# Mixed-head attention with a rational feed-forward layer: the order of the score products spread anew

## The chip, the cores and the metric

The kernel runs on one core of a Trainium2 chip. The metric is the device time in microseconds of one execution. In this document PE is TensorE's matmul stream and PEld its weight loads, DVE is VectorE, ACT is ScalarE, POOL is GpSimd, and SP is SyncE, whose queue issues most DMAs.

## The reference, cut to what matters

```python
# q, k, v: (4, 12, 448, 64); w_pre, w_post: (12, 12)
scores = scale * np.matmul(q, k.transpose(0, 1, 3, 2))
scores = np.einsum('bhij,hg->bgij', scores, w_pre)       # first mix over heads
scores = scores - np.max(scores, axis=-1, keepdims=True)
attn = np.exp(scores)
attn = attn / (np.sum(attn, axis=-1, keepdims=True) + 1e-09)
attn = np.einsum('bhij,hg->bgij', attn, w_post)          # second mix over heads
attn = np.matmul(attn, v)
# x = attn as (1792, 768); w_in: (768, 2048); w_out: (2048, 768)
h = x @ w_in
g = (a0 + a1*h + a2*h**2 + a3*h**3) / (1 + abs(b0)*abs(h) + abs(b1)*h**2 + 1e-6)
out = g @ w_out
```

All of it is in float32.

## The kernel before

**Attention.** The 448 query rows of each of the 4 batches are cut into four tiles, three of 120 rows and one of 88 (the first of batch 0, the last of the other batches), 16 tiles in all. A tile's scores are made two heads at a time: `put_qk` (line 498, weight loads and matmuls on 64x64 quarters of the array) writes a pair of heads into the two PSUM banks `ps_s`, ACT or DVE copies each head to a staging buffer `st` (helper lines 236 and 238), and a DMA from SP's queue (line 520) scatters it into `d`, where heads and ten query rows lie side by side on the partitions. There are two buffers `d`, one for even and one for odd tiles, two banks `ps_s` (one pair of heads at a time) and six staging buffers (three pairs). So a tile's six pairs are made while the tile before is worked on, and the scatter into a `d` waits until the last first mix of two tiles before has read it.

A tile is worked on in groups of two blocks of ten rows: six groups for 120 rows, five for 88. For each group g:

- `put_pre` ("pre", line 599, quarters): the first mix from `d` into a PSUM pair, `ps_t` or `ps_u`; then DVE takes the negated maximum (line 605), ACT two exps with their sums (line 614), POOL and DVE the reciprocals, and POOL scales the weights of the second mix (line 634).
- `put_post` ("post", line 674, 64x32 eighths), two groups later (`LAG = 2`): the second mix into the two banks `ps_a`, which DVE transposes into `aa` (line 690).
- `put_av` (line 739, quarters): the products of a tile with V, in three parts at groups 2, 3 and 4 of the next tile, summed in the one of `ps_t`, `ps_u` that the first mix leaves free meanwhile. For these groups, and the one behind them, the first mix has one PSUM pair only and so waits for the exps of the group before it. After the third part ACT and DVE take the sums to `xs`.

**The order.** A planner (`Plan`) takes every operation with an estimated duration and a due time (`at`), and writes out each engine's instructions in the order in which its list scheduling starts them. On TensorE it isn't free in the attention part: each call of `pe` is tied behind the one before, so the order is that of the calls. The loop over g at the end sets it: pre(g), then the score pairs in `early[g]`, then post(g-2), then AV, then the pairs in `late[g]`. `PLACES` says for a tile of five or six groups where the next tile's six pairs go: a place i is group i // 2, counted from that tile's first group, early where i is even, late where it is odd. Copies of scores go to ACT or DVE, whichever the planner finds free first.

**Feed-forward.** 64 units follow: 18 matmuls (line 918) into `ps_s`, the rational function on ACT and DVE, 18 matmuls (line 1008) into `ps_t`, `ps_u` and `ps_a`. The feed-forward weights are converted from 8-byte numbers during both parts (lines 406 to 450).

Of the kernel before, what the change touches and what calls it, by code (L numbers as in the profile page):

```python
# [54 lines left out]
class Plan:  # L55
# [11 lines left out]
    def add(self, eng, dur, fn, deps=(), at=0.0, extra=0.0, since=0.0, after=(), mode=None, late=0.0):  # L67
        op = Op(eng, dur, fn, [d for d in deps if d is not None], at, extra, since, mode, late)
        op.behind = list(after)
        self.ops.append(op)  # L70
        return op
# [124 lines left out]
def dve(n, fast=False):  # L196
    return 0.16 + 0.53e-3 * n if fast else 0.14 + 1.06e-3 * n
# [6 lines left out]
def copies(n, sb=True, on=("act", "dve")):  # L204
    return {e: act(n, sb) if e == "act" else dve(n, sb) for e in on}
# [23 lines left out]
def place(i, h):  # L229

    return STRIDE * i + EDGE + h


def move(nc, eng, o, i):
    if eng is nc.scalar:
        eng.copy(o, i)  # L236
    else:
        eng.tensor_copy(o, i)  # L238
# [3 lines left out]
def mixed_attention_then_rational_ffn(ctx: ExitStack, tc, q, k, v, w, wmix, mask, a, b2, out):  # L242
# [59 lines left out]
    tau = [T0]  # L302
# [3 lines left out]
    first = {}  # L306
# [177 lines left out]
    def put_qk(T, pr, at, ps_="s"):  # L484

        n, b = rows[T], T // 4
        box = {}

        def mm():
            if ps_ in "sa":  # L490
                box["s"] = [bank(ps_), bank(ps_)]
            else:
                pair = both(ps_)
                box["s"] = [pair[:, 0], pair[:, 1]]
            for i0, i1 in ((0, 64), (64, TQ)):
                for hh in range(2):
                    d = slice(64 * hh, 64 * hh + 64)
                    nc.tensor.matmul(  # L498
                        box["s"][hh][i0:i1, 0:S], lhsT=Q[T][d, pr, i0:i1], rhs=K[b][d, pr, :], start=True, stop=True)

        def copy(hh):
            def fn(eng):
                if T in STAGE:
                    if T not in staged:
                        t = sb[STAGE[T]].tile([128, 12 * S], F32, tag=STAGE[T], name="st0")
                        staged[T] = t.rearrange("p (h s) -> p h s", h=12)
                    box[hh] = staged[T][0:TI, 2 * pr + hh, :]
                else:
                    box[hh] = sb["st"].tile([TI, S], F32, tag="st", name="st")
                move(nc, eng, box[hh][0:n], box["s"][hh][0:n, 0:S])  # L510
            return fn

        def other(h):
            return T == 0 and h in (1, 3, 5)

        def shuffle(h):
            def fn():
                Dt[T] = d_sb[T % 2]
                p0 = place(0, h)
                (nc.scalar if other(h) else nc.sync).dma_start(  # L520
                    out=Dt[T][p0:p0 + STRIDE * (G10 - 1) + 1:STRIDE, 0:nblk[T], :], in_=box[h % 2][0:n])
            return fn

        slots = [R["ps_" + ps_].take() for _ in range(2)]
        o = pe(0.82, mm, [q_ld[T], k_ld[b][pr * len(k_ld[b]) // (H // 2)]] + slots, at=at, extra=0.16, mode="quarters")
        qk_op[T, pr] = o
        for hh in range(2):
            h = 2 * pr + hh
            home = R[STAGE.get(T, "st")]
            after = []  # L530
            if T not in STAGE or h == 0:
                free = [home.take()]
            else:
                free, after = [], [first_copy[T]]
            on = ON["s"] if T > 1 else ON["s"] if T else ("act",) if other(h) else ("dve",)
            c = add(copies(S, False, on=on), 0, copy(hh), [o, *free], at=at, after=after)
            if h == 0:
                first_copy[T] = c
            if other(h):
                c.behind.extend(shuf[0][-2:-1] if h > 1 else ())  # L540
            R["ps_" + ps_].uses[slots[hh].k].append(c)
            st_use = home.uses[0 if T in STAGE else -1]
            deps, after = [c], []
            if h == 0:
                deps += [R["d"].take(), clear[T] if T < 2 else None]
            else:
                after.append(shuf[T][0])
            if T == 1:
                after.extend(s for s in shuf[0])
            s_ = add("act" if other(h) else "sp", 0.85, shuffle(h), [x for x in deps if x], at=at - (1.0 if other(h) else 0.0), extra=0.95 * n / TI, after=after)  # L550
            st_use.append(s_)
            shuf.setdefault(T, []).append(s_)
            on_right.append(s_)
        if pr == H // 2 - 1:
            R["q"].uses[T].append(o)
        R["k"].uses[b].append(o)
# [3 lines left out]
    def pe(dur, fn, deps, at, extra, mode=None):  # L560

        op = add("pe", dur, fn, deps, at=at, extra=extra, after=pe_last[-1:], mode=mode)
        pe_last.append(op)
        return op
# [92 lines left out]
    def put_post(g, at):  # L657

        T, kb = groups[g]
        box, o4, e_use, _ = posts[g]
        nt, m = len(box), nblk[T]
        banks = [{}, {}]

        def post():
            for c in range(2):
                banks[c]["p"] = bank("a")
            for r in range(nt):
                for jh in range(2):  # L670
                    for m_ in range(2):
                        for c in range(2):
                            p, q_ = slice(64 * c, 64 * c + 64), BT * (2 * m_ + jh)
                            nc.tensor.matmul(  # L674
                                banks[c]["p"][q_:q_ + BT, JH * r:JH * (r + 1)], lhsT=box[r]["kr"][p, m_, :],
                                rhs=box[r]["e"][p, JH * jh:JH * (jh + 1)], start=True, stop=True)

        def turn(c):
            def fn():
                if kb == 0 and c == 0:  # L680
                    t = sb["a"].tile([128, NB * BT * (TI // G5)], F32, tag="a", name="aa")
                    A[T] = t.rearrange("q (b s p) -> q b s p", b=NB, p=BT)
                src = banks[c]["p"][:, 0:nt * NB * BT]
                if nt == 2:
                    o = A[T][:, :, kb + c:kb + c + m + 1:m, :].rearrange("q b r p -> q r b p")
                    src = src.rearrange("q (r b p) -> q r b p", r=2, b=NB)
                else:
                    o = A[T][:, :, c * m + kb, :]
                    src = src.rearrange("q (b p) -> q b p", b=NB)
                nc.vector.transpose(o, src)  # L690
            return fn

        slots = [R["ps_a"].take() for _ in range(2)]
        o5 = pe(0.77, post, o4 + slots, at, 0.1, "eighths")
        for u in e_use:
            u.append(o5)
        for c in range(2):
            deps, after = [o5], []
            if kb == 0 and c == 0:
                deps.append(R["a"].take())  # L700
            else:
                after.append(evac[T][0])
            o6 = add("dve", dve(nt * NB * BT), turn(c), deps, at=at + 1.0, after=after)
            R["ps_a"].uses[slots[c].k].append(o6)
            evac.setdefault(T, []).append(o6)
# [102 lines left out]
    for pr in range(H // 2):  # L808
        put_qk(1, pr, at=-2.0 + pr, ps_="uastua"[pr])
    early, late = {}, {}  # L810
    PLACES = {5: (-2, -1, 0, 2, 3, 4), 6: (-2, 0, 2, 4, 5, 6)}
    for T in range(2, NT):
        for pr, i in enumerate((-4, -3, -2, 3, 4, 5) if T == 2 else PLACES[first[T] - first[T - 1]]):
            (late if i % 2 else early).setdefault(first[T - 1] + i // 2, []).append((T, pr))
    avs = {}
    for T in range(NT):
# [9 lines left out]
    for g in range(-1, len(groups) + LAG + 4):  # L826
        if 0 <= g < len(groups):
            put_pre(g)
        for T, pr in early.get(g, ()):
            put_qk(T, pr, at=tau[g] + 0.9)  # L830
        if 0 <= g - LAG < len(groups):
            put_post(g - LAG, at=tau[g] + 1.8)
        for T, pr in avs.get(g, ()):
            put_av(T, pr, at=tau[g] + 3.6)
        for T, pr in late.get(g, ()):
            put_qk(T, pr, at=tau[g] + 3.5)
    for i in range(len(VIA) * NCV):
        g = first[1] + 6 + (first[NT - 1] - first[1] - 3) * i // (len(VIA) * NCV)
# [254 lines left out]
    for u in range(len(units)):  # L1093
        i = u + PH * NCV
# [65 lines left out]
```

## Time and profile before

| | |
|---|---|
| median of 3 runs | 833.24 us (831.55 to 838.17) |
| the profiled execution | 822.94 us, span 821.2 us |
| TensorE's granted clock, mean | 0.998 |
| PE, PEld busy | 97%, 73% of the span |
| DVE, ACT, POOL busy | 84%, 61%, 27% |
| stretch of attention | until about 340 us |

The profile is of one execution. Its times are from the start of its span. A row of the order of time merges instructions of one kind that follow each other; its start is that of the first. The place behind a bracket's arrow is what the profile takes for the event that ended the idle time before the first of them; "issue" means that no event is known.

### The profile page before, as it was taken

The numbers are of one execution on the slowest core, as the hardware profiler recorded it, in microseconds if no ns is written. First come the engines' busy times: TensorE is split into PE (matmuls) and PEld (weight loads), VectorE is DVE, ScalarE is ACT, GpSimd is POOL, SyncE is SP. The second block draws the span as 40 slices with busy tenths as digits, with TensorE's granted clock in tenths as the row PEclk, the third lists the DMA queues.
The fourth block names the chain that finished last, engine by engine and source line by source line (L and its number), as shares of the span: only waits on it lengthen the run. The fifth ranks groups of instructions, "written<-read, shape, count | busy, mean of one in ns | idle before, by whom it ended". The sixth has DMA issues, their size and how long they took to land.

```text
span 821.2 us, 23269 instructions
## 1 busy us (share of the span) xinstructions
PE 799.4 (97%) x9368; PEld 598.1 (73%) x9368; DVE 692.3 (84%) x1252; ACT 502.0 (61%) x1099; POOL 223.7 (27%) x394
## 2 busy tenths in 40 slices
PE   7899999999999999999999999999999999999998
PEld 2245555554454454689999999999999999999997
DVE  6777788888887888788999998999989998777775
ACT  2557666656665666666777776677657676545632
POOL 2334444434343445611211212222212222100000
PEclk9999999999999999999999999999999999999999
DMA  6777887668877865974733275656467534466314
GB/s 219 254 215 235 259 280 236 209 199 281 266 212 210 269 192 189 352 243 192 257 126 100 75 255 126 188 124 125 84 215 212 152 81 67 94 221 224 128 52 157
DMA packets 72332, 155.46 MB, mean 189 GB/s; under 512 B 12608, under 2 KB 53152, under 8 KB 71072
## 3 DMA queue, kind: packets, MB, share of 16 engines
q1 hardware_dynamic: 68468, 142.47, 52.6%
q0 software_dynamic: 3456, 11.01, 8.2%
q8 instruction: 74, 1.21, 0.6%
q10 hardware_dynamic: 300, 0.48, 0.2%
q14 instruction: 34, 0.28, 0.1%
HBM read 77.49 MB, written 37.75 MB: 140 GB/s over the span
## 4 chain that ended last, share of the span: by engine, by line
PE 87%; DVE 5%; DMA 3%; ACT 2%; issue 1%; POOL 1%; SPq 0%; ACTq 0%; POOLq 0%; DVEq 0%
PE ps_s L918 29%; PE ps_u L1008 10%; PE ps_t L1008 9%; PE ps_a L1008 9%; PE ps_s L498 8%; PE ps_a L674 8%; PE ps_u L599 4%; PE ps_t L599 4%; PE ps_u L739 3%; PE ps_t L739 2%; ACT e L614 2%; DVE nm L605 2%; DMA d<-st 1%; DVE aa L690 1%; DMA kk<-in_k 1%
## 5 line engine op out<-in xcount | busy, mean ns | idle before, releaser
L690 DVE STREAM_TRANSPOSE aa<-ps_a 128x448 f32<-128x448 f32 (+1 forms) x184 | 107.7, 618 | 11.7 <-PE ps_a L674 11.2
L918 PE MATMUL ps_s<-d,w 128*128 128x448 f32 x504 | 107.3, 366 | 0.0
L918 PE MATMUL ps_s<-xs,w 128*128 128x448 f32 x504 | 107.1, 366 | 0.0
L447 POOL TENSOR_TENSOR w<-cm,w 128x384 fp32r<-128x384 f32 x48 | 56.0, 1167 | 171.9 <-ACT w L236 165.0
L918 PEld LDWEIGHTS ps_s<-d,w 128*128 128x128 f32 x504 | 94.3, 188 | 8.8 <-issue 0.7
L918 PEld LDWEIGHTS ps_s<-xs,w 128*128 128x128 f32 x504 | 94.6, 188 | 7.9
L634 POOL TENSOR_SCALAR krs<-kpost,rr 128x64 f32<-128x64 f32 x180 | 80.8, 462 | 69.2 <-DVE rr L625 48.0
L674 PEld LDWEIGHTS ps_a<-e,krs 64*32 64x32 f32 x2880 | 44.9, 106 | 74.7 <-issue 26.6
L674 PE MATMUL ps_a<-e,krs 64*32 64x224 f32 x2880 | 93.2, 355 | 1.5 <-DVE aa L690 0.8
L236 ACT COPY st<-ps_s 120x448 f32<-120x448 f32 (+1 forms) x115 | 57.6, 533 | 57.8 <-PE ps_s L498 30.5
L931 ACT ACTIVATE m<-ps_s,a_sb 128x448 f32<-128x448 f32 x64 | 46.3, 723 | 76.1 <-PE ps_s L918 72.7
L498 PE MATMUL ps_s<-kk,q 64*64 64x448 f32 x696 | 90.2, 548 | 0.3 <-DVE st L238 0.3
L1008 PE MATMUL ps_u<-g,w 128*128 128x448 f32 x336 | 84.1, 366 | 0.0
L1008 PE MATMUL ps_a<-g,w 128*128 128x448 f32 x336 | 84.1, 366 | 0.0
L1008 PE MATMUL ps_t<-g,w 128*128 128x448 f32 x336 | 83.9, 366 | 0.0
L614 ACT ACTIVATE e<-ps_t,nm 128x448 f32<-128x448 f32 x92 | 57.7, 634 | 31.1 <-DVE nm L605 28.0
L614 ACT ACTIVATE e<-ps_u,nm 128x448 f32<-128x448 f32 x88 | 55.2, 633 | 28.9 <-DVE nm L605 24.6
L1008 PEld LDWEIGHTS ps_t<-g,w 128*128 128x128 f32 x336 | 63.1, 188 | 5.3
L1008 PEld LDWEIGHTS ps_a<-g,w 128*128 128x128 f32 x336 | 63.1, 188 | 5.2
L1008 PEld LDWEIGHTS ps_u<-g,w 128*128 128x128 f32 x336 | 63.1, 188 | 5.2
L961 DVE TENSOR_TENSOR sq<-sq,ua 128x448 f32<-128x448 f32 x64 | 41.4, 648 | 19.4 <-ACT ua L958 19.1
L954 ACT ACTIVATE ua<-sq 128x448 f32<-128x448 f32 x64 | 37.1, 580 | 33.9 <-DVE sq L951 33.6
(94 smaller groups left out, 1445.1 us busy)
## 6 DMA issues: line engine op xcount, KB each, us to landing
d<-st SPq DMA_DIRECT2D x144, 210.0 KB
cr<-in_w SPq DMA_DIRECT2D x64, 384.0 KB
d<-x_scr SPq DMA_DIRECT2D x5, 2688.0 KB
xs<-x_scr SPq DMA_DIRECT2D x4, 2688.0 KB
o_scr<-o POOLq DMA_DIRECT2D x24, 448.0 KB, 5.5
d<-st SPq DMA_DIRECT2D x45, 157.5 KB
x_scr<-xs SPq DMA_DIRECT2D x12, 540.0 KB
q<-in_q SPq DMA_DIRECT2D x16, 384.0 KB
```

The lines of the kernel that those rows point to most:

```text
L236: eng.copy(o, i)
L447: eng.tensor_sub(t[:, 1, :], box["m"].bitcast(F32), t[:, 0, :].bitcast(F32))
L498: nc.tensor.matmul(box["s"][hh][i0:i1, 0:S], lhsT=Q[T][d, pr, i0:i1], rhs=K[b][d, pr, :], start=True, stop=True)
L599: nc.tensor.matmul(box[r if nt == 2 else 0]["t"][64 * c:64 * c + 64, 0:S], lhsT=kpre[p], rhs=Dt[T][p, kb + c if nt == 2 else kb, :], start ...
L614: nc.scalar.activation(e, box[r]["t"][:, 0:S], AF.Exp, bias=box[0]["nm"][:, r:r + 1], accum_out=box[0]["sm"][:, r:r + 1])
L634: eng.tensor_scalar_mul(box[r]["kr"], kpost, rr)
L674: nc.tensor.matmul(banks[c]["p"][q_:q_ + BT, JH * r:JH * (r + 1)], lhsT=box[r]["kr"][p, m_, :], rhs=box[r]["e"][p, JH * jh:JH * (jh + 1)], ...
L690: nc.vector.transpose(o, src)
L918: nc.tensor.matmul(h[:, 0:S], lhsT=W[fi][:, wi, kk * 128:(kk + 1) * 128], rhs=x[:, kk // 3, xj, kk % 3, :], start=(n == 0), stop=(n == 3 * ...
L931: nc.scalar.activation(new("m"), box["h"], AF.Identity, scale=a_sb[:, 3:4], bias=a_sb[:, 2:3])
L961: nc.vector.tensor_mul(box["vv"], box["vv"], box["rc"])
L1008: nc.tensor.matmul(O[key][:, 0:S], lhsT=W[fi][:, wi, DM + m * 128:DM + (m + 1) * 128], rhs=box["g"][:, gi, :], start=(f == 0 and n == 0), ...
```

## The change

The places of the pairs of heads, given as group within the tile that is worked on (a minus counts back from its first group; a tile's pairs begin in the tile before):

| | before | after |
|---|---|---|
| six groups | -1, 0, 1, 2, 2 late, 3 | -2 late, -1, 0, 1, 2, 3 |
| five groups | -1, -1 late, 0, 1, 1 late, 2 | -2 late, -1, 0, 1, 1 late, 2 |
| tile 1 (scores of tile 2) | -2, -2 late, -1, 1 late, 2, 2 late | -2, -2 late, -1, 1, 2, 3 |

In a row of six-group tiles each group then has one pair, the fifth group's behind its AV. And a group whose predecessor has a late pair has its own early pairs behind its post instead of ahead of it, with a due time 0.9 us later.

```diff
-    PLACES = {5: (-2, -1, 0, 2, 3, 4), 6: (-2, 0, 2, 4, 5, 6)}
+    PLACES = {5: (-3, -2, 0, 2, 3, 4), 6: (-3, -2, 0, 2, 4, 6)}
     for T in range(2, NT):
-        for pr, i in enumerate((-4, -3, -2, 3, 4, 5) if T == 2 else PLACES[first[T] - first[T - 1]]):
+        for pr, i in enumerate((-4, -3, -2, 2, 4, 6) if T == 2 else PLACES[first[T] - first[T - 1]]):
             (late if i % 2 else early).setdefault(first[T - 1] + i // 2, []).append((T, pr))
...
     for g in range(-1, len(groups) + LAG + 4):
         if 0 <= g < len(groups):
             put_pre(g)
-        for T, pr in early.get(g, ()):
+        swap = g - 1 in late
+        for T, pr in () if swap else early.get(g, ()):
             put_qk(T, pr, at=tau[g] + 0.9)
         if 0 <= g - LAG < len(groups):
             put_post(g - LAG, at=tau[g] + 1.8)
+        for T, pr in early.get(g, ()) if swap else ():
+            put_qk(T, pr, at=tau[g] + 1.8)
         for T, pr in avs.get(g, ()):
             put_av(T, pr, at=tau[g] + 3.6)
         for T, pr in late.get(g, ()):
```

## Rows read from the trace of the kernel before

**Rows 1.** Stretches: a tile of attention, and 200 us of feed-forward.
```profile
core 0: us, PE busy (x) PEld busy (x) DVE busy (x) ACT busy (x) POOL busy (x), PEclk, DMA share, GB/s
75.60:96.50 20.90, 20.61 (x464) 10.35 (x456) 16.71 (x32) 14.34 (x39) 9.18 (x20) 1.00 0.77 237
...
400.00:600.00 200.00, 200.00 (x986) 184.75 (x985) 189.88 (x343) 137.04 (x260) 44.89 (x41) 1.00 0.49 138
```

**Rows 2.** Order of time, PEld: groups 0 to 5 of tile 5.
```profile
start us, us, engine line op out<-in xcount [idle before <-releaser]
117.27 0.21 PEld L599 LDWEIGHTS ps_t<-d,kpre 64*64 64x64 f32 x8 [0.36 <-PE ps_a L674]
...
122.44 0.21 PEld L599 LDWEIGHTS ps_t<-d,kpre 64*64 64x64 f32 x8 [0.36 <-ACT st L236]
...
124.10 0.56 PEld L674 LDWEIGHTS ps_a<-e,krs 64*32 64x32 f32 x32 [0.70 <-POOL krs L634]
125.02 1.47 PEld L739 LDWEIGHTS ps_u<-aa,vv 64*64 64x64 f32 x56 [0.36 <-ACT st L236]
126.44 0.25 PEld L498 LDWEIGHTS ps_s<-kk,q 64*64 64x64 f32 x8
...
129.15 0.56 PEld L674 LDWEIGHTS ps_a<-e,krs 64*32 64x32 f32 x32 [0.70 <-issue]
...
131.46 0.29 PEld L599 LDWEIGHTS ps_t<-d,kpre 64*64 64x64 f32 x8
132.46 0.14 PEld L674 LDWEIGHTS ps_a<-e,krs 64*32 64x32 f32 x2 [0.70 <-issue]
...
135.36 0.21 PEld L599 LDWEIGHTS ps_t<-d,kpre 64*64 64x64 f32 x8
...
138.26 0.24 PEld L599 LDWEIGHTS ps_u<-d,kpre 64*64 64x64 f32 x8 [0.68 <-PE ps_a L674]
```

**Rows 3.** Order of time, PEld: the same load, of group 5, in tile 10.
```profile
239.88 0.21 PEld L599 LDWEIGHTS ps_t<-d,kpre 64*64 64x64 f32 x8 [0.30 <-ACT e L614]
```

**Rows 4.** Order of time, ACT: the last exp of group 2 in rows 2.
```profile
126.25 0.22 ACT L614 ACTIVATION_READ_ACCUMULATOR e<-ps_t,nm 128x1 f32 x1
```

**Rows 5.** Order of time, PEld: pair, pre, pair at the seam to tile 11.
```profile
242.46 0.47 PEld L498 LDWEIGHTS ps_s<-kk,q 64*64 64x64 f32 x8 [0.36 <-ACT st L236]
...
244.43 0.43 PEld L498 LDWEIGHTS ps_s<-kk,q 64*64 64x64 f32 x8 [0.74 <-DVE st L238]
245.56 0.56 PEld L674 LDWEIGHTS ps_a<-e,krs 64*32 64x32 f32 x32 [0.70 <-issue]
```

**Rows 6.** Order of time, DVE and ACT: the copies at that seam.
```profile
242.64 1.17 DVE L690 STREAM_TRANSPOSE aa<-ps_a 128x448 f32<-128x448 f32 x2
243.75 0.62 DVE L238 COPY st<-ps_s 120x448 f32<-120x448 f32 x1
...
243.46 0.62 ACT L614 ACTIVATE e<-ps_t,nm 128x448 f32<-128x448 f32 x1
...
244.07 0.53 ACT L236 COPY st<-ps_s 120x448 f32<-120x448 f32 x1
```

**Rows 7.** Order of time, PEld: pair, pre, pair in the two five-group tiles.
```profile
165.40 0.44 PEld L498 LDWEIGHTS ps_s<-kk,q 64*64 64x64 f32 x8 [0.36 <-ACT st L236]
...
169.12 0.37 PEld L674 LDWEIGHTS ps_a<-e,krs 64*32 64x32 f32 x24 [0.70 <-issue]
...
249.06 0.47 PEld L498 LDWEIGHTS ps_s<-kk,q 64*64 64x64 f32 x8 [0.36 <-ACT st L236]
...
253.21 0.56 PEld L674 LDWEIGHTS ps_a<-e,krs 64*32 64x32 f32 x32 [0.70 <-POOL krs L634]
```

**Rows 8.** Order of time, PEld: pair, pre, pair in tile 1.
```profile
38.51 0.21 PEld L498 LDWEIGHTS ps_s<-kk,q 64*64 64x64 f32 x8 [0.36 <-ACT e L614]
...
41.66 0.56 PEld L674 LDWEIGHTS ps_a<-e,krs 64*32 64x32 f32 x32 [0.71 <-POOL krs L634]
```

**Rows 9.** Order of time, ACT, and the chain of waits: two waits for scatters.
```profile
251.72 0.53 ACT L236 COPY st<-ps_s 120x448 f32<-120x448 f32 x1 [1.21 <-DMA d<-st]
...
213.28 4.56 DMA d<-st
```

## The prediction

> **What bounds the kernel now.** I read three views in this order: the table of stretches, TensorE's weight loads in order of time, and DVE's and ACT's instructions at the places where those loads wait. In the feed-forward part nothing waits: TensorE is busy 200.00 of 200 us there, and the attention part is busy 20.61 of 20.90 us in a typical tile [rows 1]. So the end follows TensorE's order of work, and what the attention part gains or loses is passed on one to one to the end.
>
> The busy share hides the waits that matter. The weight loads show them, because a load that must wait starts late while earlier matmuls still stream. Attention runs in groups of two block pairs; a full group is a first mix ("pre"), a pair of heads' scores, a second mix ("post"). In the cycle of rows 2, two full groups take 122.44 - 117.27 = 5.17, or 2.58 each. Of that, pre and scores take 124.10 - 122.44 = 1.66 and post 125.02 - 124.10 = 0.92; a value product (AV) takes 126.44 - 125.02 = 1.42; a pre without scores 132.46 - 131.46 = 1.00 [rows 2]. So one pair of heads costs 0.66 us of TensorE's path in a place where nothing waits.
>
> The whole six-group cycle is 138.26 - 117.27 = 20.99. Two places of it hold waits that the change touches. (a) Pair, pre, pair in a row (from the load at 126.44 to the post at 129.15) takes 2.71, against 1.66 + 0.66 = 2.32 without a wait: 0.39 too long. Both score banks are in use, and the second pair needs the two copies of the first. (b) The group with no scores lasts 135.36 - 131.46 = 3.90, while its work is 1.00 + 0.92 + 1.42 = 3.34: 0.56 idle [rows 2]. The pre that follows takes the PSUM pair of the group before and waits for its exps; in another tile the same load shows it by name, with 0.30 us idle and "ACT e" as releaser [rows 3].
>
> By the Trainium skill (Perfetto Trace Analysis, Identifying the Most-Contended Engine) matmul busy time is a poor measure of headroom and weight-load busy time a better one. The trace agrees: the tile of rows 1 leaves 0.3 us by matmul busy time and has 10.35 of 20.90 us of weight loads. By matmul busy time the whole change could win about 4 us over 13 tiles; by the loads' starts several times that.
>
> **The change part by part.** Nothing is added or removed: the same 96 pairs, with the same matmuls, copies and scatter DMAs. In a six-group tile the pairs stood 1, 1, 2, 1, 0, 1 over groups 0 to 5; now each has one, that of group 4 behind its AV, that of group 5 behind its post. The number of changes between the mixes' two array shapes stays at 12 per tile, as each group keeps one post with other work on both sides.
>
> Six-group tiles (11 that hold a full set), each term per tile:
> - Place (a) goes: minus 0.39 [rows 2].
> - Place (b) is filled by the late pair: 3.34 + 0.66 = 4.00 against 3.90 for the same group, so the 0.56 of idle time goes and the pair nearly fits into it. Minus 0.56.
> - Groups 2 and 3 shrink to 1.66 + 0.92 + 1.42 = 4.00. But their exps bound them: the last exp of the group that began at 122.44 ends at 126.25 + 0.22 = 126.47 [rows 4], 4.03 later, and a release must still reach TensorE. I take 0.07 each: plus 0.14. Below it is zero, above it 0.5 each if copies delay the exps further.
> - The pair of group 5, now behind post, stands directly ahead of group 0's pre and pair: a new pair, pre, pair. The row that is nearest is the same place in the tiles ahead of a five-group tile, where a second pair already stood behind post of group 5: from 242.46 to 245.56 is 3.10, against 2.32, so 0.78 [rows 5]. It is long because the first pair's two copies queue behind other work: on DVE the copy at 243.75 follows two transposes (242.64, 1.17), on ACT that at 244.07 follows an exp [rows 6], and the second pair's load starts at 244.43 after 0.74 idle. In the new order these transposes and exps are also due there, so I take this row and not the 2.71 of place (a), whose copies met idle engines. Plus 0.78; bounds 0.39 (a) and 1.83 (the worst row, below).
>
> Sum: -0.39 - 0.56 + 0.14 + 0.78 = -0.03 a tile, nothing over 11 tiles. The end of the cycle stays as busy as it was: it has the late pair's copies in addition to the evacuation of the AV sums, both on ACT and DVE.
>
> Five-group tiles (2 that hold scores). Here pair, pre, pair at groups 1 and 2 is the worst of the trace: 253.21 - 249.06 = 4.15 and 169.12 - 165.40 = 3.72 [rows 7]. With group 2's pair behind post the second pair is a whole post further from the first, which leaves 2.32 for the same pieces: -1.83 and -1.40. The group without scores, which sat idle for exps, gets a pair as in (b), worth about 0.3 [rows 3] in each. Together -3.8.
>
> Tile 1 (scores of tile 2 at groups 1, 2, 3 in place of 1, 2, 2): its pair, pre, pair of 41.66 - 38.51 = 3.15 [rows 8] goes, -0.83. Its first groups stay bound by earlier scatters.
>
> The scatter DMAs: the first pair of a tile is now copied ahead of the last pre that still reads its destination, so its two scatters wait at the head of SP's queue until that pre has ended, at most the 1.66 that a pre and a pair take [rows 2]; behind them on SP stand weight and K/V loads, which have tens of us of lead. Their staging buffers are held until landing; six buffers hold three pairs, so the pair three places later must wait for them. I count 5.7 us from their issue to that pair's copies (two groups of 2.58 and part of a third), and one scatter on the chain needed 4.56 [rows 9]: zero is taken. The other end is the 1.21 us for which ACT once sat behind "DMA d<-st" [rows 9].
>
> **Total:** -0.3 - 3.8 - 0.8 = -4.9, say -5. The profiled execution lasted 822.94 us (span 821.2), so about 818 for the same execution; it lies 1.2% under the median of the runs, 833.24. The forecast is the median less 5: 828.2 us.
>
> **The rivals.** *The waits vanish:* if the new pair, pre, pair meets free engines as in (a) it costs 0.39, and the exps keep up with 4.00: -0.39 - 0.56 + 0.39 = -0.56 a tile, 6.2 over 11; the five-group tiles lose as much again as the pair costs, tile 1 its share: about -13, 820. For it: every engine but TensorE has free time in the tile (DVE 16.71, ACT 14.34 of 20.90 [rows 1]). Against it: that free time lies in groups 2 to 4, not at the tile's seam.
>
> *The seam decides (slower):* groups 5, 0 and 1 keep the length of 2.58 and now hold one pair more than groups 2 to 4 relieve. If the copies of group 5's pair come as late as in the worst row, 4.15, the new triple costs 1.83 and not 0.78, on all 11 seams: +11.5 - 5 = +6.5, or 840. It decides from 0.78 + 0.45 a tile, where the gain of 5 is used up. The copies come late at 249.06 because ACT and DVE hold mixed work there; the same would follow if SP's waiting scatters made staging late.
> In a sentence of its own: the Trainium skill (TensorEngine Tiling (Array Packing), PSUM Bottleneck) warns that packing speeds TensorE up and leaves evacuation as the limit; 0.74 us of idle load behind "DVE st" [rows 5] is such a case, and by that rule the seam would decide.
>
> *It doesn't do what it says:* DVE's and ACT's orders are made by the planner from its own durations; if it puts the copies elsewhere, the new spread shifts waits without removing any, and the time stays at 833, give or take 2.
>
> **How the numbers follow.** Forecast (825 to 831) 0.48; waits vanish (817 to 825) 0.22; no effect (831 to 835) 0.15; seam decides (835 to 845) 0.15. Range 819.5 to 838.5: it leaves out the far halves of the outer cases. One per cent is 8.3 us, about what a measurement of this kernel tells from no change (its three runs lie 0.8% apart). Below 824.9 lies the vanishing case: 0.21. Above 841.6 the far part of the seam case: 0.07. The rest, 0.72, is within 1%.
>
> **What would show it.** Right: no pair, pre, pair at groups 2 and 3; the late pair of group 4 followed by a pre without a wait on exps; groups 2 and 3 at 4.0 to 4.2; the new seam triple near 3.1; the five-group tiles some 2 us shorter each. Wrong: a seam triple over 3.5 or under 2.8; post loads that wait over 0.71 for transposes at the seam; "DMA d<-st" as releaser of copies on ACT; or waits in the feed-forward part, where I expect none.

## The result, and the profile after

The changed kernel took 836.62 us (median of 20 runs, 829.44 to 843.85), the kernel before 829.57 us (20 runs, 826.93 to 838.17): a ratio of 1.0074 [1.0055, 1.0092], so some 6 us slower where 5 us faster was forecast. The ratio leaves out executions that lie over 1.5% above the fastest of their kernel, and so it is a little below that of the two medians. The profiled execution of the changed kernel lasted 833.43 us (span 831.6), 3 us under its median; that of before, at 822.94, lay under all of its 20 runs and 7 us under their median. So of the 10.4 us between the two spans some 3 belong to the choice of the executions, and the two profiles may be compared place by place, but not by their ends.

The first view is again the table of stretches. Feed-forward is as before [rows 1]; the second row, a stop of 5 us in the attention part, has nothing like it in this stretch of the trace of before.

```profile
core 0: us, PE busy (x) PEld busy (x) DVE busy (x) ACT busy (x) POOL busy (x), PEclk, DMA share, GB/s
...
400.00:600.00 200.00, 200.00 (x983) 184.22 (x982) 190.96 (x343) 136.78 (x260) 41.62 (x39) 1.00 0.50 145
...
290.00:295.00 5.00, 2.39 (x16) 0.88 (x16) 0.56 (x1) 0.00 (x0) 0.02 (x1) 0.50 0.80 271
295.00:300.00 5.00, 5.00 (x92) 1.84 (x88) 3.32 (x8) 3.19 (x8) 1.08 (x3) 0.83 0.49 156
```

The weight loads in order of time, from the seam between tiles 5 and 6 on, answer to [rows 2] (groups inside a tile) and [rows 5] (pair, pre, pair):

```profile
start us, us, engine line op out<-in xcount [idle before <-releaser]
140.38 0.45 PEld L599 LDWEIGHTS ps_t<-d,kpre 64*64 64x64 f32 x8 [0.31 <-ACT e L614]
141.53 0.56 PEld L674 LDWEIGHTS ps_a<-e,krs 64*32 64x32 f32 x32 [0.71 <-issue]
142.45 0.21 PEld L498 LDWEIGHTS ps_s<-kk,q 64*64 64x64 f32 x8 [0.36 <-DVE xs L757]
143.90 0.21 PEld L599 LDWEIGHTS ps_u<-d,kpre 64*64 64x64 f32 x8 [1.24 <-DVE xs L757]
144.43 0.73 PEld L498 LDWEIGHTS ps_s<-kk,q 64*64 64x64 f32 x8 [0.32 <-DVE st L238]
145.87 0.80 PEld L674 LDWEIGHTS ps_a<-e,krs 64*32 64x32 f32 x32 [0.70 <-POOL sm L621]
147.02 0.21 PEld L599 LDWEIGHTS ps_t<-d,kpre 64*64 64x64 f32 x8 [0.36 <-ACT st L236]
149.60 0.21 PEld L599 LDWEIGHTS ps_u<-d,kpre 64*64 64x64 f32 x8 [0.36 <-ACT st L236]
153.62 0.25 PEld L599 LDWEIGHTS ps_u<-d,kpre 64*64 64x64 f32 x8
157.62 0.29 PEld L599 LDWEIGHTS ps_u<-d,kpre 64*64 64x64 f32 x8
161.42 0.21 PEld L599 LDWEIGHTS ps_u<-d,kpre 64*64 64x64 f32 x4 [0.16 <-issue]
```

Groups 0 to 4 begin at 143.90, 147.02, 149.60, 153.62 and 157.62. Groups 2 and 3 last 153.62 - 149.60 = 4.02 and 4.00 as forecast, and group 4, with its late pair, 3.80. The new pair, pre, pair runs from 142.45 to the post at 145.87, 3.42, and it holds a wait that the prediction did not name: pre of group 0 sits idle 1.24 us for "DVE xs L757", the second subtraction that splits the AV sums.

ACT's and DVE's order at this place says why:

```profile
140.22 0.46 ACT L236 CAST xs<-ps_u 128x360 fp32r<-128x360 f32 x1
140.96 0.53 ACT L236 COPY st<-ps_s 90x448 f32<-90x448 f32 x1 [0.28 <-PE ps_s L498]
141.38 0.46 ACT L236 CAST xs<-ps_u 128x360 fp32r<-128x360 f32 x1
...
141.88 0.53 DVE L757 TENSOR_TENSOR xs<-ps_u,xs 128x360 fp32r<-128x360 f32 x1 [0.27 <-ACT xs L236]
142.33 1.08 DVE L605 TENSOR_REDUCE nm<-ps_t 128x2 f32<-128x896 f32 x1
143.32 0.52 DVE L757 TENSOR_TENSOR xs<-ps_u,xs 128x360 fp32r<-128x360 f32 x1
```

In the kernel before the two casts, and the two subtractions, of such an evacuation stand together:

```profile
135.65 0.82 ACT L236 CAST xs<-ps_u 128x360 fp32r<-128x360 f32 x2 [0.35 <-PE ps_u L739]
136.51 0.97 DVE L757 TENSOR_TENSOR xs<-ps_u,xs 128x360 fp32r<-128x360 f32 x2 [0.69 <-ACT xs L236]
```

By the code the late pair of group 4 is due at `tau[g] + 3.5` and the evacuation of the AV sums at `tau[g] + 3.6`, in the planner's time. In the trace the pair's copy stands between the two casts on ACT, and a reduction of 1.08 between the two subtractions on DVE. The PSUM of the AV sums comes free that much later, and pre of group 0 needs it.

### The profile page after: what moved, and what is told of

Its sections match the earlier page's. It is cut to its first block, busy times and chain, and to the rows that moved or that the text cites. A ratio compares the mean times of both kernels' runs of the same rounds, so it can differ in the third digit from the quotient of the medians.

```text
span 831.6 us, 23264 instructions
## 1 busy us (share of the span) xinstructions
PE 801.3 (96%) x9368; PEld 599.9 (72%) x9368; DVE 702.7 (84%) x1266; ACT 496.9 (60%) x1085; POOL 221.6 (27%) x394
## 4 chain that ended last, share of the span: by engine, by line
PE 65%; DVE 5%; issue 1%; ACT 1%; DMA 1%; POOL 0%; SPq 0%; DVEq 0%; POOLq 0%; ACTq 0%
PE ps_s L921 26%; PE ps_u L1011 9%; PE ps_t L1011 9%; PE ps_a L1011 9%; PE ps_a L674 4%; PE ps_s L498 3%; PE ps_u L739 2%; PE ps_t L739 2%; PE ps_t L599 2%; PE ps_u L599 1%; DMA d<-st 1%; DVE ua L967 1%; DVE nm L605 1%; DVE sq L954 1%; DVE sq L964 0%
## 5 line engine op out<-in xcount | busy, mean ns | idle before, releaser
L236 ACT COPY st<-ps_s 120x448 f32<-120x448 f32 (+1 forms) x105 | 53.2, 533 | 70.0 <-issue 34.0
L614 ACT ACTIVATE e<-ps_u,nm 128x448 f32<-128x448 f32 x88 | 55.3, 635 | 27.5 <-DVE nm L605 24.5
L605 DVE TENSOR_REDUCE nm<-ps_t 128x2 f32<-128x896 f32 (+1 forms) x47 | 49.6, 1056 | 12.5 <-PE ps_t L599 12.0
```

The lines of the kernel that those rows point to most:

```text
L605: nc.vector.tensor_reduce(out=nm[:, 0:nt], in_=box[0]["both"][:, 0:nt, 0:S], axis=AX.X, op=ALU.max, negate=True)
L614: nc.scalar.activation(e, box[r]["t"][:, 0:S], AF.Exp, bias=box[0]["nm"][:, r:r + 1], accum_out=box[0]["sm"][:, r:r + 1])
```

## The experiments

All ratios are to the kernel before on the same chip. Single profiles are too coarse here: the executions of one kernel with all of its scatters lie from 6 to 22 us apart. So beside the full kernels there are "light" ones, whose score scatters move half of the columns and leave out half of the scores; their executions lie 1 to 3 us apart.

**The changed kernel again, and three parts of it.** `evac_first` makes the AV evacuation due ahead of the late pair's copies; `no_swap` leaves the second mix of a group behind its scores; `five_only` makes the change in the five-group tiles alone.

The edits of `evac_first`, `no_swap` (both on the changed kernel) and `five_only` (on the kernel before) are, in this order, with the lines between left out:

```diff
-h_ = add(copies(3 * n, False, on=ON["x_hi"]), 0, hi(hv), deps, at=at, after=after)
-l_ = add("dve", dve(3 * n), lo(hv), [h_], at=at)
+h_ = add(copies(3 * n, False, on=ON["x_hi"]), 0, hi(hv), deps, at=at - 1.5, after=after)
+l_ = add("dve", dve(3 * n), lo(hv), [h_], at=at - 1.5)
...
-swap = g - 1 in late
+swap = False
...
-    PLACES = {5: (-2, -1, 0, 2, 3, 4), 6: (-2, 0, 2, 4, 5, 6)}
+    PLACES = {5: (-3, -2, 0, 2, 3, 4), 6: (-2, 0, 2, 4, 5, 6)}
+    behind = set()
...
+            if i % 2 and first[T] - first[T - 1] == 5:
+                behind.add(first[T - 1] + i // 2 + 1)
...
-        for T, pr in early.get(g, ()):
+        swap = g in behind
+        for T, pr in () if swap else early.get(g, ()):
...
+        for T, pr in early.get(g, ()) if swap else ():
+            put_qk(T, pr, at=tau[g] + 1.8)
```

> The changed kernel once more, unaltered, for a second profile. If the losses are made by the order of the instructions, the same waits come back: the first mix of a tile waits behind DVE's second subtraction of the AV sums (0.2 to 1.24 us in nine tiles of the first profile), and the first mix after 292 us waits 5.5 us for the scatters of its tile. If they are chance of the memory traffic, the 5.5 us and the stops of 1.5 to 1.8 us in the middle of an AV stretch (50, 243 and 345 us) are gone or stand elsewhere.

Measured: 834.49 us, span 832.7, clock 0.989; the kernel before on this chip 827.67 (822.58 to 835.02). The wait for "DVE xs L757" is there again at the seams, with the same 1.24 us into tiles 5 and 6. The stop of 5.51 us is not: the seam into tile 13 takes 6.55 here and 12.07 in the first profile.

> Changed kernel with the due time of the AV sums' casts and subtractions 1.5 us earlier, so that ACT and DVE take both before the copies of the late pair. Theory 'evacuation' (the late pair's copies stand between the two casts and the reduction between the two subtractions, so the next tile's first mix waits): the waits behind DVE's subtraction, some 4.4 us beyond the usual 0.22 each, go, the seam triple falls from about 3.2 to 2.9, and the ratio to the kernel before falls from 1.007 to about 1.001. Theory 'memory traffic' (late scatters and code blocks make the loss): ratio stays at 1.005 to 1.009. My recorded rival, the copies of group 5's pair: the triple stays at 3.2 and the ratio falls by less than 0.002.

Measured: 830.38, ratio 1.0043 [1.0010, 1.0076]. The loss isn't gone. Whether it is smaller can't be told here, as the interval overlaps that of the change (1.0055 to 1.0092); the light kernels below can tell.

> Changed kernel with every early pair ahead of post again; only the places differ from the kernel before. Recorded view (the pair of group 5 ahead of post meets the late pair of group 4 as pair, pre, pair, and the seam is free): triple moves to group 4/5 with about 3.1, ratio within 0.003 of the changed kernel's 1.007. Theory 'evacuation': the late pair's copies must then be ready even earlier, so the waits stay, 1.006 to 1.012. If the swap itself is the loss: back to 1.000 or below.

Measured: 831.16, ratio 1.0021 [0.9990, 1.0053]. Without the swap the loss can't be told from none here, which made the swap a suspect.

> Kernel before with only the two five-group tiles' places changed (and their pairs behind post); six-group tiles and tile 1 as before. By my recorded sum: 3.8 us shorter, ratio 0.9954. If the gain of those tiles is eaten by the copies of the added late pair at the seam ahead of them: ratio 0.999 to 1.001. If the loss of the change lies in these tiles: over 1.003.

Measured: 826.63, ratio 1.0000 [0.9969, 1.0030]. The interval leaves room for a gain of 2.6 us at most, so the 3.8 us that the prediction took from these two tiles are not there.

**Less traffic, and another place for the odd pair.** `before_again` is the kernel before. `light_before` and `light_after` have the halved scatter. `gap4` is `five_only` with the lines of `evac_first`, and with only the first pair of a six-group tile moved, to a late place in group 4 of the tile before; groups 5 and 0 then have no new pair, pre, pair.

The edit of every light kernel, and then the line in which `gap4` differs from `five_only` beside those of `evac_first`:

```diff
-                    out=Dt[T][p0:p0 + STRIDE * (G10 - 1) + 1:STRIDE, 0:nblk[T], :], in_=box[h % 2][0:n])
+                    out=Dt[T][p0:p0 + STRIDE * (G10 - 1) + 1:STRIDE, 0:nblk[T], 0:S // 2], in_=box[h % 2][0:n, 0:S // 2])
...
-    PLACES = {5: (-3, -2, 0, 2, 3, 4), 6: (-2, 0, 2, 4, 5, 6)}
+    PLACES = {5: (-3, -2, 0, 2, 3, 4), 6: (-3, 0, 2, 4, 5, 6)}
```

> The kernel before once more, unaltered, for a second profile. Both theories expect the lengths of its groups to come back to 0.1 us where nothing but the order of the instructions counts (six-group tile 20.5 to 21). Theory 'memory traffic': its first profile was a lucky execution (822.9 us against a median of 828), so this one shows some 5 us of stops that the first has not, in the middle of AV stretches or ahead of a first mix, but fewer than the 9 to 11 us above the floor that both profiles of the changed kernel have.

Measured: 840.54 in the profiled execution, span 838.8, clock 0.990; its other runs here have a median of 829.84 (825.01 to 838.51). By the starts of the groups' pre loads tiles 2, 8, 10 and 11 last 24.77, 24.44, 23.76 and 24.34 us in it, against 20.96, 20.56, 21.50 and 20.10 in the profile of before. So the kernel before has long tiles too, and its first profile, faster than all of its 20 runs, shows few of them; the tile of [rows 1] is an undisturbed one.

> Kernel before with every scatter of scores moving only the first half of the columns: same instructions and order, half of the scatters' bytes; the other half of the scores is left at what the buffer held, so the output is not the reference's. Theory 'memory traffic': stops shrink, some 4 us faster than the kernel before (ratio 0.993 to 0.997). If the stops have nothing to do with traffic: 0.999 to 1.001.

Measured: 813.57 (812.97 to 814.88), ratio 0.9811 [0.9771, 0.9852], span 812.0: 16 us under the kernel before, some four times what was expected.

> Changed kernel with the same halved scatters (half of the scores left out). Theory 'memory traffic' (the new spread loses its time to late scatters and code blocks): 8 to 10 us faster than the changed kernel, so its distance to the halved kernel before falls from 0.7% to 0.2% or less. If the loss lies in the order on ACT and DVE: the distance stays at 0.5% to 0.8%.

Measured: 819.33 (817.77 to 819.95), ratio 0.9876 [0.9834, 0.9917], span 817.3: with little spread between its runs the change still costs 819.33 - 813.57 = 5.8 us, so the order itself is slower. Both kernels at one seam, by the weight loads:

```profile
129.19 0.21 PEld L599 LDWEIGHTS ps_t<-d,kpre 64*64 64x64 f32 x8
131.77 0.21 PEld L599 LDWEIGHTS ps_u<-d,kpre 64*64 64x64 f32 x8 [0.36 <-PE ps_a L674]
134.37 0.21 PEld L599 LDWEIGHTS ps_t<-d,kpre 64*64 64x64 f32 x8 [0.36 <-ACT st L236]
```

```profile
132.42 0.45 PEld L599 LDWEIGHTS ps_t<-d,kpre 64*64 64x64 f32 x8 [0.30 <-ACT e L614]
134.49 0.21 PEld L498 LDWEIGHTS ps_s<-kk,q 64*64 64x64 f32 x8 [0.36 <-issue]
135.93 0.21 PEld L599 LDWEIGHTS ps_u<-d,kpre 64*64 64x64 f32 x8 [1.24 <-DVE xs L757]
...
139.05 0.21 PEld L599 LDWEIGHTS ps_t<-d,kpre 64*64 64x64 f32 x8 [0.36 <-ACT st L236]
```

Groups 5 and 0 take 134.37 - 129.19 = 5.18 before and 139.05 - 132.42 = 6.63 after. Over the nine seams between six-group tiles, tile 1 included, the means are 5.16 and 6.43; over the eleven six-group tiles groups 2 to 4 go from 12.83 to 12.16.

> A version from the readings: six-group tiles as before, but the pair of group 5 goes one group ahead, behind the AV of group 4, where the kernel before sits idle (places -2 late, 0, 1, 2, 2 late, 3; no pair beside the seam, so no new pair, pre, pair); five-group tiles as in the change; AV sums evacuated first. By the groups' lengths group 5 falls from 2.58 to 1.92 and group 4 grows from 3.71 to 3.79, 0.58 a tile, 6.4 over 11 tiles, and the five-group tiles give 2.3: ratio 0.989 to 0.993 if only the order counts. Theory 'memory traffic': the first scatters wait for the last first mix as in the change, stops grow by some 5 us, ratio 0.996 to 1.002.

Measured: 829.42, ratio 1.0004 [0.9972, 1.0035]. With no new pair, pre, pair at the seam no loss shows, but no gain either, where the lengths of its groups had promised 0.989 to 0.993.

**The parts, with the halved scatter.** Another chip; the kernel before took 826.64 there.

> Halved scatters (half of the scores left out) with the changed order and the AV sums evacuated first. The halved kernels measured 813.6 (before) and 819.3 (changed) with next to no scatter between runs, so the loss is in the order. Theory 'seam': groups 5 and 0 last 6.4 in place of 5.16 us, some 1.0 for the pair, pre, pair and up to 0.5 more for the split evacuation; this kernel takes only the second away: about 4 us faster than the halved changed kernel, 815 to 816, and no first mix waits behind DVE's second subtraction. If the split evacuation costs nothing: 819. If it is all: 813.5 or below.

Measured: 814.68, ratio 0.9844 [0.9815, 0.9873], span 813.9.

> Halved scatters (half of the scores left out) with the new places, every early pair ahead of post. Theory 'seam': the pair of group 5 then stands behind the late pair and the pre, the triple only moves from groups 5/0 to 4/5; from the unhalved runs the seam is 5.9 to 6.1 us, so 815 to 817. If the position behind post is the whole loss: 813 or below.

Measured: 809.94, ratio 0.9789 [0.9765, 0.9814], span 807.2. That is below the 815 to 817 that the theory of the seam gave.

> Halved scatters (half of the scores left out) with only the two five-group tiles changed. My recorded sum gave 3.8 us; without scatter waits the two tiles of the halved kernel before are already 18.83 and 19.25 us, and the halved changed kernel's are 19.19 and 20.08. Recorded sum: 809.8. Theory 'the recorded gain was waits for scatters, which the order doesn't remove': 813 to 814.

Measured: 814.19, ratio 0.9839 [0.9813, 0.9864], span 813.1: no gain in the five-group tiles with little scatter either.

> Halved scatters (half of the scores left out) with the version that moves group 5's pair into the idle time of group 4 and leaves none at the seam. Theory 'seam': seam 4.8 to 5.0 in place of 5.16, groups 2 to 4 as before, so 0.2 to 0.35 a tile, 810 to 812. If the first scatters' wait for the last pre costs by itself: 813.6 or more.

Measured: 811.75, ratio 0.9811 [0.9786, 0.9836], span 809.0.

The seam in `light_evac_first` and then in `light_no_swap`:

```profile
132.77 0.46 PEld L599 LDWEIGHTS ps_t<-d,kpre 64*64 64x64 f32 x8 [0.30 <-ACT e L614]
134.85 0.21 PEld L498 LDWEIGHTS ps_s<-kk,q 64*64 64x64 f32 x8 [0.36 <-issue]
135.28 0.15 PEld L599 LDWEIGHTS ps_u<-d,kpre 64*64 64x64 f32 x4 [0.22 <-issue]
136.51 0.29 PEld L498 LDWEIGHTS ps_s<-kk,q 64*64 64x64 f32 x8 [0.70 <-ACT st L236]
138.60 0.21 PEld L599 LDWEIGHTS ps_t<-d,kpre 64*64 64x64 f32 x8 [0.36 <-ACT st L236]
```

```profile
127.82 0.46 PEld L599 LDWEIGHTS ps_t<-d,kpre 64*64 64x64 f32 x8 [0.30 <-ACT e L614]
...
131.34 0.21 PEld L599 LDWEIGHTS ps_u<-d,kpre 64*64 64x64 f32 x8 [0.84 <-DVE xs L757]
133.92 0.21 PEld L599 LDWEIGHTS ps_t<-d,kpre 64*64 64x64 f32 x8 [0.36 <-ACT st L236]
```

With the evacuation first the wait of 1.24 is gone and the seam is 138.60 - 132.77 = 5.83; the pair, pre, pair now waits 0.70 for a copy instead. Without the swap group 5's pair stands ahead of its post. A wait for the evacuation is left here, 0.84, but group 0 is a plain 2.58, and the seam takes 133.92 - 127.82 = 6.10. Over the nine seams the mean is 6.43 with the change, 6.03 with the evacuation first and 5.85 without the swap. Evacuation first gives back 819.33 - 814.68 = 4.7 us; the medians are from two chips, but the starts of the loads say the same (tiles 2 to 14 take 270.84 and 266.41 us). It leaves 0.4 to 1.1 us to the two runs of the light kernel before (814.31 and 813.57), which is about the distance between these two. Without the swap these tiles take 262.43, against 266.51 in `light_before`: with the halved scatter the new places alone are a gain.

**The full kernels against the halved, on one chip.** The kernel before took 828.09 there (822.65 to 844.23). These four put to the test whether the swap alone is the loss.

> The changed kernel, unaltered, beside the same kernel without the swap on one chip. Theory 'swap' (the pair put behind post is what costs; the new places alone don't): 1.006 to 1.009 of the kernel before, and 4 us or more over the kernel without the swap.

Measured: 836.14, ratio 1.0107 [1.0065, 1.0149], span 834.3.

> New places, every early pair ahead of post, unhalved. Theory 'swap': 0.995 to 1.002 of the kernel before, at least 4 us under the changed kernel. Theory 'places' (the first scatters' wait for the last pre, or the denser traffic behind it, costs by itself): 1.003 or more, within 3 us of the changed kernel.

Measured: 834.12 (828.64 to 840.51), ratio 1.0087 [1.0053, 1.0120], span 835.7, clock 0.987.

> Kernel before with halved scatters (half of the scores left out), again, now on the same chip as the next: 813 to 815.

Measured: 814.31, ratio 0.9853 [0.9827, 0.9878], span 814.3.

> Halved scatters (half of the scores left out), new places without the swap, on the same chip as the halved kernel before. Theory 'swap': 3 to 4 us under it, as the two lay apart on two chips (809.9 and 813.6). If that was the chips: within 1 us of it.

Measured: 810.65, ratio 0.9801 [0.9774, 0.9828], span 807.7.

The theory of the swap falls for the full kernel: with half of the scatter the places without it gain 814.31 - 810.65 = 3.7 us, with all of it they lose 834.12 - 828.09 = 6.0 on the same chip. Leaving the swap out takes 836.14 - 834.12 = 2.0 off there and 4.4 by the first ratios (836.62 x (1 - 1.0021/1.0074)). The intervals just miss each other by the first ratios (1.0055 and 1.0053) and overlap here, and the two runs without the swap, 1.0021 and 1.0087, hardly agree. So its part in the full kernel is known no better than as nothing to some 4 us. Full scatter costs the kernel before 14 us on this chip and the new places without the swap 23.5.

No kernel of the study beats the kernel before: `five_only` and `gap4` are equal to it, and what `gap4` may gain with half of the scatter (811.75, against 813.57 and 814.31 for `light_before`, each on another chip) does not show with all of it.

## Why the prediction was wrong

The measured 836.62 lies inside the stated range, 819.5 to 838.5. That is no support for the sum: the time went up by 6 where the sum had it go down by 5, and the base of the forecast, a median of three runs, lay 833.24 - 829.57 = 3.7 us above that of twenty.

**What held.** The end follows TensorE's order: feed-forward has 200.00 of 200 us busy after as before. Places (a) and (b) are gone: groups 2 to 4 lose 12.83 - 12.16 = 0.67 a tile with the halved scatter, where -0.39 - 0.56 + 0.14 = -0.81 was forecast. Tile 1's groups 0 to 4 gave 17.54 - 16.68 = 0.86 between the two light kernels (0.83 forecast).

**The step that failed first: the seam's +0.78.** Groups 5 and 0 grew by 6.43 - 5.16 = 1.27 in the mean of the nine seams. The term was priced by the triple alone, 3.10 against 2.32. The triple came out at 2.87 to 3.58, 3.24 in the mean of the light kernel, close to the forecast, but for another reason: with the evacuation first it is 2.84. So 0.40 of it is the evacuation of the AV sums, which the prediction named as sharing ACT and DVE with the late pair, and then gave no price; it is split by that pair's copies, and pre of group 0 waits for it. Five of the nine seams of `light_after` hold a wait of 0.67 to 1.25 for "DVE xs" and take 6.55 in the mean; the other four wait 0.22 to 0.25, as `light_evac_first` also does, and take 6.29. `light_evac_first` shows the evacuation's part by taking it away: 0.40 a seam, 1.1 and 0.7 at the two seams behind five-group tiles, 4.7 us in all.

What it leaves, 6.03 - 5.16 = 0.87, is near the 0.78, in part by luck: its triple costs 0.52, and the rest stands beside the triple, where the prediction looked for nothing (from pre of group 5 to its post 1.22 in place of 1.00, and 1.06 in place of 0.92 behind the last post). The point from which the seam decides, 0.78 + 0.45 = 1.23 a tile, was just passed, and the gain that was to be used up there was not made elsewhere either. The rival "the seam decides" had the place and the sign; its price, 1.83, and its mechanism, late copies of group 5's pair, were not what happened. The rival "it doesn't do what it says" had the planner's order as the danger, but no loss from it.

**The step that failed second: five-group tiles, -3.8.** The two rows of 4.15 and 3.72 [rows 7] were read as waits of the order. Part of them was waits for scatters: the group of tile 11 that holds the 4.15 lasts 6.08 in the profile of before and 5.27 with half of the scatter, that of tile 7, which holds the 3.72, 5.63 and 4.78. With half of it the two tiles take 18.83 and 19.25 before and 19.19 and 20.08 after, a loss of 1.2 us; the profiles with all of it gave 20.18 and 20.10 against 19.18 and 20.03, a gain of 1.1. What group 2 gained went back in groups 3 and 4. The starts of groups 2, 3 and 4 of tile 11 and of the next tile, in `light_before` and then in `light_after`:

```profile
241.33 0.79 PEld L599 LDWEIGHTS ps_u<-d,kpre 64*64 64x64 f32 x8
246.60 0.21 PEld L599 LDWEIGHTS ps_u<-d,kpre 64*64 64x64 f32 x8 [0.20 <-ACT e L614]
250.25 0.14 PEld L599 LDWEIGHTS ps_u<-d,kpre 64*64 64x64 f32 x2 [0.35 <-ACT e L614]
...
254.22 0.32 PEld L599 LDWEIGHTS ps_u<-d,kpre 64*64 64x64 f32 x8
```

```profile
244.30 0.75 PEld L599 LDWEIGHTS ps_u<-d,kpre 64*64 64x64 f32 x8
248.84 0.25 PEld L599 LDWEIGHTS ps_u<-d,kpre 64*64 64x64 f32 x8
253.49 0.19 PEld L599 LDWEIGHTS ps_u<-d,kpre 64*64 64x64 f32 x2 [0.19 <-issue]
...
257.83 0.32 PEld L599 LDWEIGHTS ps_u<-d,kpre 64*64 64x64 f32 x8
```

Group 2 goes from 5.27 to 4.54, group 3 from 3.65 to 4.65 and group 4 from 3.97 to 4.34. So group 2 gave up 0.73 where 1.83 was forecast, and in tile 7 it gave up 4.78 - 4.58 = 0.20 where 1.40 was. In `light_after` group 3 also holds a late pair, which the places of the six-group tile behind it put there. `light_five_only` tells the two apart, as it has no pair there. Its group 3 of the same tile:

```profile
247.13 0.25 PEld L599 LDWEIGHTS ps_u<-d,kpre 64*64 64x64 f32 x8
248.37 0.14 PEld L674 LDWEIGHTS ps_a<-e,krs 64*32 64x32 f32 x2 [0.99 <-POOL krs L634]
...
251.27 0.20 PEld L599 LDWEIGHTS ps_u<-d,kpre 64*64 64x64 f32 x3
```

It lasts 4.14 without the late pair, so about half of the 1.00 that this group 3 grew by comes with group 2's pair behind its post: post now waits 0.99 for the scaled weights, 0.70 before. In tile 7 that half is missing (3.71 before, 3.70 in `light_five_only`). The late pair adds the other 0.51, less than its 0.66, and in tile 7 it adds 3.77 - 3.70 = 0.07. So it does fill idle time, as forecast. The 0.37 of group 4 is not in `light_five_only` (4.04 and, in tile 7, 3.98), so it belongs to the six-group places.

**Tiles 2 and 3** were counted with the other nine and gained nothing at groups 2 to 4 (13.15 before and 13.22 after in tile 2, 13.15 and 13.30 in tile 3, halved scatter): weight preparation runs beside them there. By the trace, though no run tested it, this holds them: DVE waits 1.44 us for a clamp of that preparation on POOL, the reduction stands behind it, and the next pre waits 1.49 for its exps, here in tile 3 of the changed kernel, on DVE and among the weight loads:

```profile
88.05 0.36 DVE L420 TENSOR_SCALAR cm<-cm 128x384 int32<-128x384 int32 x1 [1.44 <-POOL cm L416]
...
89.19 1.08 DVE L605 TENSOR_REDUCE nm<-ps_t 128x2 f32<-128x896 f32 x1
...
92.20 0.21 PEld L599 LDWEIGHTS ps_t<-d,kpre 64*64 64x64 f32 x8 [1.49 <-ACT e L614]
```

Added up with half of the scatter, term by term: the eleven seams into six-group tiles cost 12.7 us where 8.6 was forecast, groups 2 to 4 give 7.3 where 8.9 was, and the five-group tiles with the seams ahead of them give 0.4 where 3.8 was. The three differences make 9.1 of the 10.2 us between the forecast of -4.9 and the 5.3 between the spans of 812.0 and 817.3.

**The step whose failure is only half explained: "zero is taken" for the scatters.** For the change itself they add up to some 3 us: it loses 5.8 us with half of the scatter and 6 to 9 with all (ratios 1.0074 and 1.0107). For the new places without the swap they add 10 us on one chip, from a gain of 3.7 to a loss of 6.0. One bound of the prediction is shown to be wrong: a first scatter was to wait for the last pre at most 1.66 us, and at the seam into tile 7 it waits 3.68 to 3.69 in all three profiles of the changed kernel. But it waits as long in `light_after`, and that seam got no longer, 6.60 before and 6.52 after, so it cost nothing there. The staging buffers are not it either: in the profile of after the score copies waited 0.4 us for "DMA d<-st" in all, and 11.9 us in that of `before_again`.

In the traces two kinds of stop stand out that the order of work doesn't call for. Here are the chain of waits and the weight load at one place of the profile of after, then a load in it and the same one in `again`:

```profile
280.94 8.78 DMA d<-st
289.71 2.89 issue
...
292.58 0.33 PEld L599 LDWEIGHTS ps_t<-d,kpre 64*64 64x64 f32 x8 [5.51 <-issue]
...
100.31 0.13 PEld L498 LDWEIGHTS ps_s<-kk,q 64*64 64x64 f32 x1 [1.54 <-issue]
...
105.12 0.13 PEld L498 LDWEIGHTS ps_s<-kk,q 64*64 64x64 f32 x1 [1.24 <-issue]
```

The load at 292.58 stands behind a late scatter, but the scatter's part ends at 289.71, and for the 2.89 us that follow the chain names no releaser (the last section comes back to them). The load at 100.31 stands for the other kind, a stop inside a run of loads that waits for nothing in the profile. Of these, over 1.0 us long, there is one in the attention part of the profile of before (1.77 at 281.80), but five in `before_again` and four in `five_only`; there are four or five in each profile of the changed kernel, five in each without the swap, and one to three with the halved scatter. So halving the scatter thins them out, but their number doesn't tell the changed kernel from the kernel before, and that they are the 10 us is not shown. One place does recur: tile 3 takes 23.8 to 24.5 us in all six profiles with the new places and all of the scatter, 21.6 to 22.1 with half, and 20.9 and 21.1 in the two of the kernel before; the stop in its group 5 is in all four of these six that have the swap. Why full scatter costs more there is open, and so is the rest of the 10 us: around the stop at 100.31 the DMA engines were 0.57 busy (99.5 to 100.5), less than the 0.75 of the whole attention part.

## What to carry to other kernels

Price an inserted step by the whole group it joins, and look up in the planner which work is due at nearly the same time. Here the new step stood in the middle of an evacuation, not beside it, and the wait landed on the next to need that PSUM. A row from one execution is a property of the order only if its repetitions in other tiles have it too: the rows of the five-group tiles, 3.8 of the 4.9 us here, held waits that belong in part to transfers. Nor does the count of stops in one profile speak for a kernel: two profiles of the kernel before had one and five. Where a kernel's executions scatter more than the effect, halve the bytes of the suspected transfer: that took the spread of the runs here from some 12 us to 2 and showed which part of the loss is the order's and which is not.

## What the runs showed of the hardware

TensorE's loads stopped inside a run of one kind, with no releaser in the profile, for 1.0 to 2.8 us, 50 times in the attention parts of the 18 profiles. Each time they went on 1.3 to 1.8 us after a 16 KB transfer on the queue of instructions had ended, for example at 100.31 after 98.77 in the profile of after and at 281.80 after 280.28 in that of before. With half of the score scatter there were one to three of these stops in a profile, in the others up to five. The long stop that ends at 292.58 is of both kinds: such a transfer ended at 291.00, 1.58 us ahead of the load.

Around the idle 5.51 us the granted clock of the stretch 290 to 295 was 0.50, the lower of the two levels (1.2 GHz), and 0.83 in the mean of the next 5 us, so this stop was paid for a second time. Halving the score scatter alone, 19 of 155 MB, took 14 us from the kernel before on one chip and 16 on another, though the DMA engines' share in the attention part only went from 0.75 to 0.61.
